# Attention's scores taken in float32 on halves of the array's rows, with TensorE's order written by hand

## The chip, the core and the metric

The kernel runs on one core of a Trainium2 chip. A core has TensorE (PE, the matrix array; its weight loads are shown as PEld), VectorE (DVE), ScalarE (ACT), GpSimd (POOL) and SyncE (SP, which here issues nearly all DMAs). The metric is the device time of one launch in microseconds (us).

## The reference

Three stages follow one another; everything is float32.

```python
# attention: B, H, S, D = 2, 8, 576, 64
scores = q @ k^T / sqrt(D)
x = log1p(|i-j|) / log1p(max(i, 1))          # depends on positions only
bias = relu(x * w1 + b1) @ w2                # hidden 32, one value per head
attn = softmax(scores + bias); out = attn @ v
# x = the heads side by side: (1152, 512)
# MoE: each token goes to its argmax expert of 8 (a capacity of 288 each):
y = relu(x @ w1[e]) @ w2[e], times the gate's probability
# a second layer: h = y @ w_in (512 -> 2048), leaky relu with alpha, @ w_out
```

## The kernel before

**Units.** Attention is done in 16 units (`pair(i)`): a pair of heads of one batch, and a set of query rows. Units 0 to 7 (phase 0) have two "big" row blocks of 128 rows (`ul` 0 and 1) and a "small" block in which 64 rows of both heads share the 128 partitions. Units 8 to 15 (phase 1) have the two big blocks alone. The big block has 576 keys for each of two heads. The list `UL` holds, in this order: the small blocks of units 0 to 2, their ul 0, their ul 1 (nine steps), then units 3 to 7, each big and then small, then units 8 to 15. The loop over `s` puts into one step the scores of entry s, the transposes of entry s - 1 and the values of entry s - 2.

**Scores.** `load(i)` brings q and k of a pair of heads, each stored twice over the partitions. `split(i)` makes of each a rounded part (DVE casts, L224 and L229) and a remainder (POOL subtracts, L225 and L230) in the type fp32r. `big(h, ul)` then forms the 128 x 576 scores of one head in four fp32r matmuls of 288 columns over all 128 rows of the array (L290); the two parts stand one above the other in those rows. The small block takes eight such matmuls (L274).

**Softmax and values.** `soft` adds the bias and takes the maximum in one DVE instruction (L262) and the exponential on ACT (L264). `stage_transpose` turns the result over on PE (L327, small: L309 and L314) in groups of up to four 128 x 128 blocks, `(0, 1)`, `(2, 3)`, `(4,)`, `(5, 6)`, `(7, 8)`, into one of two PSUM banks (`pt`); a copy by ACT or DVE (L298, L300) brings each group to SBUF. `stage_values` multiplies by v on halves of the array's columns (L352), and by `vd` over the whole array (L355).

**Bias.** There are 36 bias tiles k. Each needs four tensors `h` (128 x n, n from 576 down to 304; L169 on ACT, L171 on DVE or POOL, by `H_PLAN`), matmuls on four column tiles of the array (L175), an eviction in two instructions to `st` (L182 on ACT, L184 on DVE, by `EV_PLAN`), and a DMA into DRAM (`bd`). `load_bias` reads it back in the layout of the scores. Thirteen tiles are written ahead of the first scores (`PRE0` and `NB[0]`), the rest in the nine first steps and in units 3 to 7.

**PSUM.** The pool `pq` has two tiles of two banks each, for scores and bias tiles alike; `pt` and `pa` have two banks each.

**Order.** Each engine runs its own queue in order. The code above sets which work is written first, and a scheduler then chooses each engine's order from its own estimates. Behind attention come the routing (L406 and on, started in pieces when unit 11's values are done, `late`), the gather of the tokens by POOL (L495), the experts' products (L611 and on), and the second layer (L845 and L857).

## Time and profile before

| | |
|---|---|
| median of three runs | 421.54 us (421.21 to 425.41) |
| the profiled execution | 422.72 us |
| its span, first to last instruction | 421.0 us |
| mean granted clock of TensorE | 0.986 of 2.4 GHz |
| busy: PE, DVE, ACT, POOL | 94%, 75%, 57%, 27% of the span |

The busy shares are means over the whole span. Attention and what follows it have different limits, so the rows below are taken stage by stage.

### The profile page before, as it was taken

The page shows a single profiled execution, that of the slowest core. Times are in us where ns is not written, and L with a number is a line of the kernel's source. Part 1 is how long each engine was busy: PE and PEld are TensorE (multiplying, and loading weights), DVE is VectorE, ACT ScalarE, POOL GpSimd, SP SyncE. Part 2 cuts the span into 40 slices and gives each one's busy share as a digit, 9 for nine tenths or more (in the row PEclk, how much of TensorE's full clock was granted, in tenths as well). Part 3 has the DMA queues.
Part 4 walks back from the last instruction along what each step waited for, and adds up shares of the span by engine and source line. Part 5 has one row for each costly group of instructions (what it writes and reads, how often), then busy time and mean ns, then how long its engine had stood idle before and what let it go on. Part 6 is the DMA issues. An engine that isn't in the chain of part 4 may idle for free. (4 is left out here: it accounts for less than half of the span.)

```text
span 421.0 us, 7767 instructions
## 1 busy us (share of the span) xinstructions
PE 394.4 (94%) x2710; PEld 294.6 (70%) x2711; DVE 316.5 (75%) x723; ACT 239.4 (57%) x515; POOL 113.5 (27%) x99
## 2 busy tenths in 40 slices
PE   4689999989999999999998989999999999999993
PEld 2234544535787877786764789887898989897982
DVE  5889777697678777595977799832799998998440
ACT  4556646767666667566456333633577665665531
POOL 5732002342255556655242054001000000000003
PEclk9789999999999999999999999999999999999997
DMA  8847777777896889976149729929345644651003
GB/s 249 233 128 197 219 225 221 221 191 223 251 290 216 263 246 309 303 265 206 36 139 250 245 105 272 293 104 298 91 148 166 195 137 167 200 158 44 2 0 125
DMA packets 58059, 80.29 MB, mean 191 GB/s; under 512 B 10935, under 2 KB 37687, under 8 KB 58012
## 3 DMA queue, kind: packets, MB, share of 16 engines
q1 hardware_dynamic: 56828, 77.24, 60.5%
q0 software_dynamic: 1184, 2.48, 1.6%
q8 instruction: 23, 0.38, 0.4%
q14 instruction: 24, 0.20, 0.1%
HBM read 61.01 MB, written 20.09 MB: 193 GB/s over the span
## 5 line engine op out<-in xcount | busy, mean ns | idle before, releaser
L264 ACT ACTIVATE p<-p,mn 128x576 f32<-128x576 f32 x72 | 55.8, 775 | 32.6 <-DVE mn L262 32.1
L175 PE MATMUL bps<-h,c 128*32 128x512 f32 (+17 forms) x352 | 60.6, 520 | 13.4 <-DVE h L171 13.3
L171 DVE TENSOR_SCALAR h<-c 128x432 f32<-128x432 f32 (+17 forms) x108 | 54.5, 555 | 9.3 <-PE bps L175 9.1
L262 DVE CUSTOM_DVE_ANT_0 p<-sps,bias 128x576 f32<-128x576 f32 x72 | 53.7, 754 | 9.8 <-PE sps L290 5.2
L230 POOL TENSOR_TENSOR kk<-kr,kk 64x1216 fp32r<-64x1216 f32 x16 | 44.7, 2796 | 8.1 <-issue 6.3
L327 PE MATMUL t<-ident,p 128*128 128x128 f32 x288 | 46.0, 279 | 0.4 <-ACT PT L298 0.4
L175 PEld LDWEIGHTS bps<-h,c 128*32 128x32 f32 x352 | 17.1, 116 | 39.0 <-DVE h L171 17.3
L352 PE MATMUL av<-PT,vt 128*64 128x256 f32 (+1 forms) x304 | 42.8, 357 | 0.0
L327 PEld LDWEIGHTS t<-ident,p 128*128 128x128 f32 x288 | 32.9, 141 | 13.9 <-issue 5.5
L290 PE MATMUL sps<-kk,qh 128*128 128x288 f32 x120 | 39.4, 344 | 0.3 <-ACT st L182 0.3
L225 POOL TENSOR_TENSOR ql<-qr,qh 128x512 fp32r<-128x512 f32 x15 | 23.7, 1583 | 58.7 <-DVE qh L224 40.8
L298 ACT COPY PT<-t 128x512 f32<-128x512 f32 x51 | 29.0, 579 | 16.3 <-PE t L327 16.0
L889 POOL DMA_INDIRECT out<-orow,ti x5 | 4.9, 973 | 116.7 <-ACT orow L886 115.2
L845 PE MATMUL fg<-yh,w1h 128*128 128x304 f32 x120 | 36.3, 302 | 0.0
L845 PE MATMUL fg<-yh,w1l 128*128 128x304 f32 x120 | 36.2, 302 | 0.0
L845 PE MATMUL fg<-yl,w1h 128*128 128x304 f32 x120 | 36.2, 302 | 0.0
L182 ACT ACTIVATE st<-bps,c 128x527 f32<-128x527 f32 (+57 forms) x58 | 26.2, 501 | 16.2 <-PE bps L175 11.7
L290 PE MATMUL sps<-kk,ql 128*128 128x288 f32 x120 | 33.9, 298 | 0.0
L352 PEld LDWEIGHTS av<-PT,vt 128*64 128x64 f32 x304 | 21.2, 136 | 13.1 <-issue 7.5
L857 PE MATMUL facc<-w2h,hl 128*128 128x512 f32 (+1 forms) x75 | 29.8, 398 | 0.3 <-DVE hl L547 0.3
L857 PE MATMUL facc<-w2h,hh 128*128 128x512 f32 (+1 forms) x75 | 29.7, 396 | 0.0
L770 ACT ACTIVATE cv<-d 128x512 f32<-128x512 f32 x32 | 21.5, 675 | 14.1 <-DMA d<-in_win 7.2
(216 smaller groups left out, 927.4 us busy)
## 6 DMA issues: line engine op xcount, KB each, us to landing
bd<-st SPq DMA_DIRECT2D x36, 295.5 KB, 3.2
kr<-in_kT SPq DMA_DIRECT2D x16, 608.0 KB, 5.8
raw<-in_ew SPq DMA_DIRECT2D x16, 512.0 KB, 6.2
d<-in_win SPq DMA_DIRECT2D x16, 512.0 KB, 3.7
d<-in_wout SPq DMA_DIRECT2D x16, 512.0 KB, 3.7
bias<-bd SPq DMA_DIRECT2D x16, 288.0 KB, 4.6
vt<-in_vt SPq DMA_DIRECT2D x16, 256.0 KB, 4.7
bias<-bd SPq DMA_DIRECT2D x16, 256.0 KB, 4.3
```

The costliest lines, as they stand in the source:

```text
L171: (G if plan[c] == 'P' else V).tensor_scalar(h, tab[:, :n], psi[:, i:i + 1], 0.0, ALU.add, ALU.max)
L175: T.matmul(ps[32 * c:32 * c + 32, n0:n1], w2n, hs[c][:, n0:n1], start=True, stop=True)
L182: A.activation(d, src, AF.Copy, scale=rr[:, t:t + 1])
L230: G.tensor_tensor(kk[64:128], k[64:128], kk[64:128].bitcast(F32), ALU.subtract)
L262: V.tensor_tensor_reduce(out.rearrange("p (a b) -> p a b", a=2), ps[:, :, :288], bias.rearrange("p (a b) -> p a b", a=2), -0.125, 3.0e38, ...
L264: A.activation(out, out, AF.Exp, bias=mn, scale=-1.0, accum_out=acc)
L290: T.matmul(ps[:, nh, :288], qs[j][:, h, 128 * ul:128 * ul + 128], kk[:, k0:k0 + 288], start=j == 0, stop=j == 1)
L298: A.copy(o, i)
L327: T.transpose(t[:, jl, 128 * i:128 * i + 128], u.P[ul][:, 128 * j:128 * j + 128], ident)
L352: T.matmul(u.o[64 * h:64 * h + 64, :n], v[:, j, 64 * h:64 * h + 64], rhs(h, j), start=j == 0, stop=False, skip_group_check=True)
L845: T.matmul(ps, w[:, 128 * k:128 * k + 128], x[:, k, s], start=k + i == 0, stop=k + i == 5)
L857: T.matmul(acc[i][:m], h[:, r:r + m], w, start=f == 0 and j == 0, stop=f == NF - 1 and j == 2)
```

## The change

**Scores.** `split` is gone, with all casts and subtracts. q (128 x 320) and k (128 x 640) are loaded once, head 0 on partitions 0 to 63 and head 1 on 64 to 127, half the bytes of before. `big(ul)` forms the scores of both heads: four float32 matmuls of 288 columns, each over half of the array's rows (64), written so that one on the upper half is followed by one on the lower half; the heads go to two PSUM tiles (four banks). The small block does the same with 64 x 64 tiles of the array, both halves into one bank on different partitions.

**Bias.** `bias_h` writes the four `h` of a tile two tiles ahead (twelve buffers instead of six), all on DVE but one of eight up to tile 13, which ACT makes. All evictions are ACT's, and each stands right behind its tile's matmuls. `NB` and `EV` spread tiles and loads anew: `PRE0` 9 tiles, then 2, 2, 2, 3, 3, 3, 1, 1, 1 in the first nine steps, then 2 in each of units 3 to 7. There, one tile lies behind the transposes and one behind the values.

**Order.** `course()` is written under a manual schedule for PE: PE's order is the order of the code, `do()` by `do()`. The other engines stay with the scheduler. Big and small of one unit are one step (`SL`). The pieces of the routing are spread over more places. v has five buffers instead of four.

```diff
-H_PLAN = '322211000000016221010166000066000000'
-EV_PLAN = 'AAAAAAAAAAADAADDDDAAAAADAAAAAAAAAAAD'
-NB = (4, 0, 2, 4, 4, 3)
-EV = {0: [(0, 4, 1)], 1: [(1, 2)], 2: [(0, 0, 0)], 5: [(0, 0, 1), (0, 1, 1)], 6: [(0, 1, 0)]}
+NB = (2, 2, 2, 3, 3, 3, 1, 1, 1, 2, 2, 2, 2, 2)
+EV = {0: [(4, 1)], 2: [(0, 0)], 3: [(0, 1)], 5: [(1, 0), (1, 1)]}
...
+
+        def bias_h(k):
+
             t = (list(range(32, 36)) + list(range(32)))[k]
-            ps = pq.tile([128, 1024], F32, tag="pq", name="bps")
-            plan = ('DDDA', 'DDDD', 'DDAA', 'DADA', 'DAAA', 'PDDA', 'PDDD')[int(H_PLAN[k])]
-            hs = []
+            n = max(S - 16 * t, 16 * t + 16)
             for c in range(4):
-                h = bp.tile([128, S], F32, tag="h", name="h", bufs=6)[:, :n]
+                h = bp.tile([128, S], F32, tag="h", name="h", bufs=12)[:, :n]
                 i = t * 4 + c
-                if plan[c] == 'A':
+                if c == 3 and k % 2 == 0 and k < 14:
                     A.activation(h, tab[:, :n], AF.Relu, bias=psi[:, i:i + 1], scale=1.0)
                 else:
-                    (G if plan[c] == 'P' else V).tensor_scalar(h, tab[:, :n], psi[:, i:i + 1], 0.0, ALU.add, ALU.max)
-                hs.append(h)
+                    V.tensor_scalar(h, tab[:, :n], psi[:, i:i + 1], 0.0, ALU.add, ALU.max)
+                HS[k][2].append(h)
+
+        def bias_t(k):
+            if k == 0:
+                bias_h(0)
+                bias_h(1)
+            if k + 2 < NT:
+                bias_h(k + 2)
+            t, n, hs = HS.pop(k)
+            nf, nr = S - 16 * t, 16 * t + 15
+            ps = pq.tile([128, 1024], F32, tag="pq", name="bps")
             for n0, n1 in ((0, min(n, 512)), (512, n)):
                 for c in range(4 if n1 > n0 else 0):
                     T.matmul(ps[32 * c:32 * c + 32, n0:n1], w2n, hs[c][:, n0:n1], start=True, stop=True)
...
-                    d = st[:, o:o + src.shape[1]]
-                    if EV_PLAN[k % len(EV_PLAN)] == 'A':
-                        A.activation(d, src, AF.Copy, scale=rr[:, t:t + 1])
-                    else:
-                        V.tensor_scalar(d, src, rr[:, t:t + 1], None, ALU.mult)
...
-            pend.append(finish)
-            if len(pend) > 1:
-                pend.pop(0)()
+            st = bp.tile([128, PITCH], F32, tag="st", name="st", bufs=4)
+            for o, src in ((0, ps[:, nr:0:-1]), (nr, ps[:, 0:nf])):
+                A.activation(st[:, o:o + src.shape[1]], src, AF.Copy, scale=rr[:, t:t + 1])
...
-        RAW, KQV = {}, {}
...
-            q = kq.tile([128, 2, 320], F32, tag="qr", name="qr")[:, :, :w]
-            k = kq.tile([128, 1216], F32, tag="kr", name="kr")
-            v = ap.tile([128, 4, 128], F32, tag="vt", name="vt", bufs=4)
-            SY.dma_start(q, a["qT"][b, hp][:, :, 320 * ph:320 * ph + w])
+            q = kq.tile([128, 320], F32, tag="qr", name="qr", bufs=4)[:, :w]
+            k = kq.tile([128, 640], F32, tag="kr", name="kr", bufs=4)
+            v = ap.tile([128, 4, 128], F32, tag="vt", name="vt", bufs=5)
...
-        def split(i):
...
-                    V.tensor_copy(hi, x)
-                    G.tensor_tensor(lo, x, hi.bitcast(F32), ALU.subtract)
-
-            kk = (kq.tile([128, 1216], F32R, tag="bias", name="kk", bufs=9) if 2 <= i < EP else
-                  kq.tile([128, 1216], F32R, tag="kk", name="kk"))
-            V.tensor_copy(kk, k)
-            G.tensor_tensor(kk[64:128], k[64:128], kk[64:128].bitcast(F32), ALU.subtract)
-            KQV[i] = qs, kk, v
+            KQV[i] = q, k, v
...
-                unit(i, 1)
-            unit(i, 0)
+            return u
+
+
+        SL = [[unit(i, not uls, uls)] for uls in ((), (0,), (1,)) for i in range(EP)]
+        SL += [[unit(i, z) for z in ((0, 1) if i < 8 else (0,))] for i in range(EP, 16)]
 
         def soft(ps, bias, out, acc):
...
                 ps = pq.tile([128, 2, 512], F32, tag="pq", name="sps")
                 for nh in range(2):
-                    for n, (h, j) in enumerate(((0, 0), (0, 1), (1, 0), (1, 1))):
-                        k0 = 640 * h + 288 * nh
-                        T.matmul(ps[:, nh, :288], qz[u.i % 2][j][:, 2 * h:2 * h + 2], kk[:, k0:k0 + 288],
-                                 start=n == 0, stop=n == 3)
+                    for p in half:
+                        T.matmul(ps[p, nh, :288], q[p, 0:64], k[p, 64 + 288 * nh:352 + 288 * nh], start=True, stop=True)
...
-            def big(h, ul):
-                ps = pq.tile([128, 2, 512], F32, tag="pq", name="sps")
+            def big(ul):
+                ps = [pq.tile([128, 2, 512], F32, tag="pq", name="sps") for _ in range(2)]
+                c = q.shape[1] - 256 + 128 * ul
                 for nh in range(2):
-                    for j in range(2):
-                        k0 = 576 * h + 288 * nh
-                        T.matmul(ps[:, nh, :288], qs[j][:, h, 128 * ul:128 * ul + 128], kk[:, k0:k0 + 288], start=j == 0, stop=j == 1)
+                    for h, p in enumerate(half):
+                        k0 = 64 - 64 * h + 288 * nh
+                        T.matmul(ps[h][:, nh, :288], q[p, c:c + 128], k[p, k0:k0 + 288], start=True, stop=True)
                 row = 2 * u.ph + ul
-                soft(ps, BT[row, u.hp][:, h], u.P[ul][:, h * S:h * S + S], rs[u.b][:, row, 2 * u.hp + h:2 * u.hp + h + 1])
-
-            return [lambda h=h, ul=ul: big(h, ul) for h in range(2) for ul in u.uls]
+                for h in range(2):
+                    soft(ps[h], BT[row, u.hp][:, h], u.P[ul][:, h * S:h * S + S],
+                         rs[u.b][:, row, 2 * u.hp + h:2 * u.hp + h + 1])
+
+            return [lambda ul=ul: big(ul) for ul in u.uls]
...
-            tr = stage_transpose(UL[s - 1]) if 1 <= s <= NU else []
-            va = stage_values(UL[s - 2]) if s >= 2 else []
+                tr = sum(map(stage_transpose, ws), [])
+                va = sum(map(stage_values, xs), [])
+                nb = NB[s] if s < len(NB) else 0
...
+                do(tr)
+                do(sc)
+                if len(sc) == 2:
+                    do(tr, 3)
+                    more_bias(1)
+                    do(sc[1:])
+                    do(tr, 9)
+                    do(sc)
+                    do(va, 99)
+                    more_bias(nb - 1)
+                elif sc:
+                    step()
+                    do(tr, 2)
+                    step()
+                    do(va, 99)
+                    step()
+                    do(sc)
+                    do(tr, 9)
+                    step()
+                else:
+                    step()
+                    do(tr, 9)
+                    step()
+                    more_bias(nb and 1)
+                    do(va, 99)
+                    more_bias(nb - 1)
...
+                if xs and xs[0].i == 11:
+                    st = routing(0)
+                    late.extend([st[0:1], st[1:2], st[2:3], st[3:5], st[5:7], st[7:9], st[9:10], [st[10], st[11], second]])
+
+        with tc.manual_schedule(engines={ET.PE}):
+            course()
+        while late:
+            for f in late.pop(0):
+                f()
```

The names in the order below: `sps` are scores in PSUM, `t` transposed blocks in PSUM, `p` the softmax's result, `av` the values, `qh` and `ql` the rounded part and the remainder of q, `qr` and `kr` q and k as loaded. Square brackets tell whose work an instruction waits for (`DVE_49`: DVE's, `DMAHW`: a DMA's).

PE, in the last eight units (8 to 15), one unit before:

```order
L355 MATMUL av<-PT,vd_98 128x256
L290 MATMUL sps<-kk,qh 128x288
L290 MATMUL sps<-kk,ql 128x288
L290 MATMUL sps<-kk,qh 128x288
L290 MATMUL sps<-kk,ql 128x288
L327 MATMUL t_2113<-ident,p_1966 128x128
...
L290 MATMUL sps<-kk,qh 128x288
L327 MATMUL t_2166<-ident,p_2058 128x128
...
L290 MATMUL sps<-kk,ql 128x288
...
L352 MATMUL av<-PT,vt 64x256 x7
L355 MATMUL av<-PT,vd_98 128x256
L290 MATMUL sps<-kk,qh 128x288
```

PE, the same place after (`p_1760` is what the unit before left, `p_1848` and `p_1849` are ul 0 and ul 1 of this one):

```order
L323 MATMUL av<-PT,vt 64x256 x7
L326 MATMUL av<-PT,vd_98 128x256
L259 MATMUL sps<-kr,qr 128x288 [waits DVE_49] x2
L259 MATMUL sps<-kr,qr 128x288 x2
L298 MATMUL t_1908<-ident,p_1760 128x128 [waits DVE_49]
...
L298 MATMUL t_1914<-ident,p_1760 128x128 [waits Activation_49]
...
L298 MATMUL t_1934<-ident,p_1848 128x128 [waits DVE_49]
L298 MATMUL t_1934<-ident,p_1849 128x128 [waits Activation_49]
...
L259 MATMUL sps<-kr,qr 128x288 [waits DMAHW4_49,DMAHW3_49]
L259 MATMUL sps<-kr,qr 128x288 x3
```

Before, a head's scores stood between groups of transposes, one head at a time. Now both heads of a row block stand together, the second block behind the values, and four transposes of this unit's own softmax stand ahead of the next unit's scores.

DVE, in the last eight units, before and then after:

```order
L262 ISA p_2058,mn<-sps,bias 128x576
L262 ISA mn 128x1
L300 COPY xT_110<-av 128x256
L262 ISA p_2059,mn<-sps,bias 128x576
L262 ISA mn 128x1
L300 COPY PT<-t_2113 128x256
L262 ISA p_2058,mn<-sps,bias 128x576
L262 ISA mn 128x1
L262 ISA p_2059,mn<-sps,bias 128x576
L262 ISA mn 128x1
L300 COPY PT<-t_2139 128x512
L224 CAST qh<-qr 128x512
```

```order
L230 ISA p_1849,mn<-sps,bias 128x576
L230 ISA mn 128x1
L230 ISA p_1849,mn<-sps,bias 128x576
L230 ISA mn 128x1
L271 COPY PT<-t_1914 128x512
L230 ISA p_1925,mn<-sps,bias 128x576
L230 ISA mn 128x1
L230 ISA p_1925,mn<-sps,bias 128x576
L230 ISA mn 128x1
L271 COPY PT<-t_1958 128x256
L271 COPY xT_102<-av 128x256
```

Behind the second block's two `p_1849` now stands the copy of four transposed blocks (`t_1914`), which the next transposes need, since there are two banks for them; the casts of q and k are gone.

DVE, from the start to the first softmax, before and then after:

```order
L171 TENSOR_SCALAR h<-c_84 128x528 x2
L171 TENSOR_SCALAR h<-c_84 128x544 x2
L224 CAST qh<-qr 128x512
L229 CAST kk<-kr 128x1216
L171 TENSOR_SCALAR h<-c_84 128x560 x2
L224 CAST qh<-qr 128x512
L224 CAST qz_102<-qr 128x2x64
L224 CAST qz_104<-qr 128x2x64
L229 CAST kk<-kr 128x1216
...
L171 TENSOR_SCALAR h<-c_84 128x432 x4
L262 ISA p_439,mn<-sps,bias_354 128x576
```

```order
L163 TENSOR_SCALAR h<-c_84 128x528 x3
L163 TENSOR_SCALAR h<-c_84 128x544 x4
L163 TENSOR_SCALAR h<-c_84 128x560 x3
L163 TENSOR_SCALAR h<-c_84 128x576 x7
...
L163 TENSOR_SCALAR h<-c_84 128x448 x3
L163 TENSOR_SCALAR h<-c_84 128x432 x4
L230 ISA p_369,mn<-sps,bias_356 128x576
L230 ISA mn 128x1
L230 ISA p_421,mn<-sps,bias_356 128x576
L230 ISA mn 128x1
```

Before, 41 `h` and eight casts stand ahead of the first `p`; after, 49 `h` and no cast.

## Rows read from the trace of the kernel before

**Rows 1.** Busy time by stage: start:end, us, engines' busy time, PE clock, DMA share, GB/s.

```profile
core 0: us, PE busy (x) PEld busy (x) DVE busy (x) ACT busy (x) POOL busy (x), PEclk, DMA share, GB/s
0.00:39.00 39.00, 27.43 (x169) 10.51 (x170) 30.73 (x54) 20.68 (x40) 18.32 (x31) 0.91 0.68 197
39.00:106.70 67.70, 65.40 (x465) 33.66 (x465) 52.83 (x139) 44.07 (x94) 19.08 (x15) 1.00 0.79 219
106.70:153.00 46.30, 46.29 (x390) 37.28 (x388) 34.13 (x88) 28.61 (x67) 20.95 (x17) 1.00 0.81 257
153.00:228.00 75.00, 74.56 (x524) 54.27 (x522) 56.07 (x154) 45.69 (x101) 35.66 (x19) 1.00 0.69 218
228.00:421.00 193.00, 180.68 (x1172) 158.87 (x1170) 142.76 (x293) 100.38 (x214) 19.48 (x19) 0.99 0.49 153
```

**Rows 2.** Timeline of DVE, front: start, us, engine, line, operation [idle before].

```profile
5.42 1.72 DVE L171 TENSOR_SCALAR h<-c 128x528 f32<-128x528 f32 x4
...
12.05 2.83 DVE L229 CAST kk<-kr 128x1216 fp32r<-128x1216 f32 x1 [1.12 <-DMA kr<-in_kT]
14.80 7.21 DVE L171 TENSOR_SCALAR h<-c 128x576 f32<-128x576 f32 x8
...
40.30 0.76 DVE L262 CUSTOM_DVE_ANT_0 p<-sps,bias 128x576 f32<-128x576 f32 x1
```

**Rows 3.** Timeline of POOL, front.

```profile
16.71 2.85 POOL L230 TENSOR_TENSOR kk<-kr,kk 64x1216 fp32r<-64x1216 f32 x1
```

**Rows 4.** Timeline of PE: four places from the first transposes to unit 8's scores.

```profile
42.12 0.66 PE L309 MATMUL t<-ident,p 128*128 128x128 f32 x4
...
55.93 0.37 PE L290 MATMUL sps<-kk,qh 128*128 128x288 f32 x1
...
104.52 0.77 PE L290 MATMUL sps<-kk,qs 128*128 128x288 f32 x4
...
153.12 0.40 PE L290 MATMUL sps<-kk,qh 128*128 128x288 f32 x1
```

**Rows 5.** DMA issues: KB each, median us from issue to landing.

```profile
bd<-st SPq DMA_DIRECT2D x36, 295.5 KB, 3.2
...
bias<-bd SPq DMA_DIRECT2D x16, 288.0 KB, 4.6
```

**Rows 6.** Timeline of ACT, front: an eviction.

```profile
39.05 0.91 ACT L182 ACTIVATE st<-bps,c 128x143 f32<-128x143 f32 x2 [1.03 <-PE bps L175]
```

**Rows 7.** Timeline of PE, phase 0: a bias tile, then eight transposes and two heads' scores.

```profile
111.03 1.06 PE L175 MATMUL bps<-h,c 128*32 128x512 f32 x8
112.02 0.40 PE L290 MATMUL sps<-kk,qh 128*128 128x288 f32 x1
...
126.73 1.07 PE L327 MATMUL t<-ident,p 128*128 128x128 f32 x8
127.56 0.38 PE L290 MATMUL sps<-kk,qh 128*128 128x288 f32 x1
...
128.79 0.66 PE L309 MATMUL t<-ident,p 128*128 128x128 f32 x4
```

**Rows 8.** Timeline of PE, one unit of the last eight.

```profile
170.34 0.70 PE L355 MATMUL av<-PT,vd 128*128 128x256 f32 x2
170.69 0.48 PE L290 MATMUL sps<-kk,qh 128*128 128x288 f32 x1
...
176.05 1.94 PE L352 MATMUL av<-PT,vt 128*64 128x256 f32 x14
177.92 0.70 PE L355 MATMUL av<-PT,vd 128*128 128x256 f32 x2
178.27 0.48 PE L290 MATMUL sps<-kk,qh 128*128 128x288 f32 x1
```

**Rows 9.** Timelines of PE, DVE and ACT, from one head's last score matmul on.

```profile
171.27 0.29 PE L290 MATMUL sps<-kk,ql 128*128 128x288 f32 x1
171.71 0.76 DVE L262 CUSTOM_DVE_ANT_0 p<-sps,bias 128x576 f32<-128x576 f32 x1 [0.21 <-PE sps L290]
...
174.14 0.69 DVE L300 COPY PT<-t 128x512 f32<-128x512 f32 x1
...
172.51 0.78 ACT L264 ACTIVATE p<-p,mn 128x576 f32<-128x576 f32 x1 [2.58 <-DVE mn L262]
173.19 0.18 ACT L264 ACTIVATION_READ_ACCUMULATOR p<-p,mn 128x1 f32 x1
173.28 0.56 ACT L298 COPY PT<-t 128x512 f32<-128x512 f32 x1
```

**Rows 10.** Timelines of POOL and PE, attention's end.

```profile
216.84 0.98 POOL L495 DMA_INDIRECT xd<-xr,ci  x1 [0.30 <-issue]
...
227.87 0.74 PE L593 MATMUL xjT<-ident,xj 96*128 96x96 f32 x7
...
231.63 0.53 PE L611 MATMUL g<-xh,w1h 128*128 128x288 f32 x2
```

More of the change, by code (lines that the diff above doesn't have):

```diff
@@ L106, in build @@
             G.memset(vd[b], 0.0)
-        qz = [[bp.tile([128, 4, 64], F32R, name=f"qz{i}{j}") for j in range(2)] for i in range(2)]
-        for z in qz[0] + qz[1]:
-            G.memset(z.bitcast(F32), 0.0)
         xT = [xp.tile([128, 4, 640], F32, tag=f"xT{b}", name=f"xT{b}") for b in range(B)]
@@ L248, in unit @@
             u.last = small == 0 and 1 in uls
-            UL.append(u)
-        for uls in ((), (0,), (1,)):
-            for i in range(EP):
-                unit(i, not uls, uls)
-        for i in range(EP, 16):
-            if i < 8:
-                unit(i, 1)
-            unit(i, 0)
+            return u
+        SL = [[unit(i, not uls, uls)] for uls in ((), (0,), (1,)) for i in range(EP)]
+        SL += [[unit(i, z) for z in ((0, 1) if i < 8 else (0,))] for i in range(EP, 16)]
         def soft(ps, bias, out, acc):
@@ L266, in stage_scores @@
         def stage_scores(u):
-            qs, kk, _ = KQV[u.i]
+            q, k, _ = KQV[u.i]
+            half = [slice(64 * h, 64 * h + 64) for h in range(2)]
             def small():
@@ new lines, in course, with do, step @@
+        def course():
+            nonlocal raw
+            for k in range(PRE0):
+                more_bias(1)
+                if k in (1, 3):
+                    load(2 + k // 2)
+            load_bias(4, 0)
+            load_vd(1)
+            for s in range(NU + 2):
+                us, ws, xs = [SL[z] if 0 <= z < NU else [] for z in (s, s - 1, s - 2)]
+                u = us[0] if us else None
+                for x in EV.get(s, ()):
+                    load_bias(*x)
+                if u and u.i < 8 and u.last and u.i % 2 == 0 and u.hp < 3:
+                    if u.i > 0:
+                        for w in (0, 1):
+                            load_bias(w, u.hp + 1)
+                    if u.hp < 2:
+                        load_bias(4, u.hp + 2)
+                if u and u.i == 7:
+                    load_bias(2, 0)
+                    load_bias(2, 1)
+                if u and 8 <= u.i < 11:
+                    load_bias(3, u.hp + 1)
+                    if u.hp < 2:
+                        load_bias(2, u.hp + 2)
+                if u and u.i == 2 and u.small:
+                    SY.dma_start(c1, a["c1"])
+                if u and 8 <= u.i < 15:
+                    clear(3 * u.i - 24)
+                sc = sum(map(stage_scores, us), [])
+                if u and u.last and u.i + 2 < 16 and u.i + 2 not in KQV:
+                    load(u.i + 2)
+                tr = sum(map(stage_transpose, ws), [])
+                va = sum(map(stage_values, xs), [])
+                nb = NB[s] if s < len(NB) else 0
+                def do(fs, n=1):
+                    for f in fs[:n]:
+                        f()
+                    del fs[:n]
+                def step():
+                    if late:
+                        for f in late.pop(0):
[4 more added lines that the diff above has]
+                    do(tr, 3)
+                    more_bias(1)
+                    do(sc[1:])
[19 more added lines that the diff above has]
+                    more_bias(nb - 1)
+                if u and u.i == 7:
+                    load_bias(3, 0)
+                if raw is None and u and u.i == 8:
+                    for b in range(B):
+                        rest_sums(b)
+                if xs and xs[0].i == 8:
+                    right.close()
+                    raw = ctx.enter_context(tc.tile_pool(name="raw", bufs=1, side="right"))
+                if xs and xs[0].i == 11:
+                    st = routing(0)
+                    late.extend([st[0:1], st[1:2], st[2:3], st[3:5], st[5:7], st[7:9], st[9:10], [st[10], st[11], second]])
```

107 lines of the change are left out of this document (15 added, 92 removed).

## Prediction

> **What bounds the kernel now.** I read the busy time by stage first [rows 1]. It shows two limits. From 39 us on PE is the engine that sets the pace: 65.40 of 67.70 us busy, then 46.29 of 46.30, then 74.56 of 75.00. In the first 39 us it is busy for 27.43 only, at a granted clock of 0.91, and DVE for 30.73. So work taken from DVE and POOL can pay in the first 39 us directly, and behind that only where PE gets less to do. The last 193 us are not touched by the change. They start when the tokens of attention are routed, so a gain in attention counts as far as it reaches the first job's product.
>
> The timeline of DVE's front shows what holds the start [rows 2]. Four h of 528 columns took 1.72 us, .43 each. The eight of 576 columns took 7.21 us, .90 each, and one cast of k took 2.83 us. Both lie beside POOL's subtract, of which one took 2.85 us [rows 3]. The first softmax came at 40.30, the first transposes at 42.12, the first wide scores at 55.93, unit 2's last scores at 104.5, unit 8's first at 153.1 [rows 2, 4]. These are the marks that I move one after the other.
>
> **The front.** Before the first softmax DVE now has 49 h and no cast, and POOL subtracts nothing. Undisturbed h of 576 to 432 columns, from .43 for 528 columns [rows 2], are some .40 each: 49 x .40 = 19.6 us from 5.4, so DVE is free at 25.0. The softmax needs the small bias, which is stored and read back: eviction, store and load took .91, 3.2 and 4.6 us [rows 5, 6], its tiles are the first four, and its read stands behind five later stores in SP's queue. I allow 1.3 us for that: the first softmax at 26.3, the first transposes 1.9 behind it as before, at 28.2 instead of 42.12: 14 us gained. The big blocks' bias for unit 0 ends with tile 12, evicted near 32.6; 3.2 + 4.6 later, at about 41, the first wide softmax can run, against some 56: 15 us gained.
>
> The six steps behind that hold three bias tiles in each of the first three, one in each of the others. In the first three ACT is the longest chain: two exponentials of .78 + .18 [rows 9], a copy of .56, three evictions of .91 [rows 6] and the hand-over to the next scores, which need the second PSUM tile, make 7.1 us each. The other three take 5.3 each by the same sum with one eviction and PE's own waits. Unit 2's last scores would end at 41 + 3 x 7.1 + 2 x 5.3 = 72.9, against 105.2 [rows 4]: 32 us gained. Part of this is work put off: ten of 36 bias tiles are left for later.
>
> **What scores cost on PE.** A float32 matmul of 256 columns on the whole array takes two passes of some .215 us: `vd`'s two ran from 177.92 to 178.27 with the change of shape [rows 8], and fourteen passes of `av`, in pairs on two column halves at once, lie in 1.87 us. For 288 columns that is .48. Two heads on row halves at once make two pairs for each block, .97 us. Before, two heads took eight fp32r matmuls in 1.2 us (127.56 to 128.79 [rows 7]), each .13. So the scores cost PE about the same, if the halves run at once; no row of before has row halves. The nearest rows, `av` on column halves, say that they do, and I take that. The other bound is one after the other, 1.93 us for a block.
>
> The Trainium skill speaks for it too ("TensorE: Matmul & The Clock Gate", Part 3): matmuls on different row groups run concurrently, and four row tiles gave 3.07 times the speed of one. Were two halves to reach that 77%, a pair would take .63 us instead of .48, and 64 pairs on the path would add some 9 us, 423 in all: an estimate from that page, which no run here shows.
>
> Of those 1.87 us, one `av` matmul alone and three pairs are 4 x .43 = 1.72; the rest, .15, is a change of the array's shape. I take .16. The order counts 160 of them in attention on either side, so they cancel.
>
> **Units 3 to 7.** PE's work in one is: scores 1.92, small 2 x .48 = .96, 23 transposes of .104 (eight in .83 [rows 7]) 2.4, values 1.72 + .43, `vd` .53, twelve changes 1.9, two bias tiles of .75 (.99 at 512 columns [rows 7], less for fewer) 1.5: 11.5 us. To this come waits that the hand-written order makes. The second transposes wait for a copy that stands behind two softmax instructions of .76 on DVE; the small block's last transpose waits in the same way; the next unit's scores wait until ACT has evicted the bias tile. From these durations [rows 6, 9] I count 1.2 to 1.4, .5 and .4. The five units then take 10.1, 11.7, 13.8, 13.8 and 12.5 us, the first ones with fewer tiles and cover from work left over. With 5.3 for the step before, unit 8's first scores come at about 140, against 153.1: of 32 us, 19 are given back here, and 13 to 14 stay.
>
> **The last eight units.** Before, a unit took 7.58 us, which is PE's work with hardly a gap: from `vd` at 170.34 to `vd` at 177.92 [rows 8]. After: scores 1.92, 18 transposes 1.9, values 1.72, `vd` .43, six changes .96, together 6.9. But the next unit's first four transposes now need the exponential of this unit's second block, and a bank that DVE's copy frees behind two softmax instructions. Counted from the last score matmul: the first softmax ends .44 + .76 after that matmul's start, the second .75 later, the copy .69 after that [rows 9]. PE has only the eight transposes, .83 us [rows 7], to put between. That leaves about 1.3 us without work. I take 8.3 us for a unit, 9.1 and 9.3 for the first two, where the pipeline turns from one kind of unit to the other; against 7.58 that loses 5.6 in the eight and some 3 more with the two slow ones and the routing pieces. Attention would end at 219.5 instead of about 227.9, a gain of 8.4. Behind its end the gather and its transposes lie open (216.84, then 227.87 and 231.63 [rows 10]); since routing starts behind the same unit and less attention covers it, I charge 1.5. The first product comes at 224.7 instead of 231.6: 7 us gained.
>
> The casts, subtracts and half of q's and k's bytes that are gone beyond the front count for nothing: POOL was no engine that PE waited for there, and DMA was busy for 0.69 to 0.81 of the stages [rows 1]. If that cover is wrong, it is a gain.
>
> **Sum.** 422.72, the profiled execution, less 7 is 415.7. It stood 1.2 above the median, so I predict 414 us (-1.8%). A change of under 1%, 4.2 us, can't be told from none here.
>
> **Rivals.**
> First, the row halves run one after the other. Then each pair costs .48 more. 80 pairs make 38.4; those of the front partly lie beside ACT's chain, so some 32 count, and the time is 414 + 32 = 446. It decides from .09 more per pair on, since 7 / 80 = .09 uses up the gain. For it: no row shows row halves, and both heads' weights must be loaded into one array. Against it: the column halves run at once in every unit.
>
> Second, the waits of the hand-written order don't appear, since DVE and ACT are free (56 and 46 of 75 us busy [rows 1]) and choose an order that I did not follow closely enough. Then PE's work alone counts: 1.3 x 8 + 1.8 in the last eight, 5.6 in units 3 to 7, some 5 in the three slow steps of the front: 23 us less, 391.
>
> Third, the small block's two halves write one PSUM bank and are held apart: 16 pairs x .48 = 7.7, so 422, no change. Against it: four column tiles write one bank at once in each bias tile (eight passes in .99 [rows 7]). The Trainium skill has this as a rule ("TensorEngine Tiling (Array Packing)", Restrictions and Gotchas): different row tiles cannot access the same PSUM bank at the same time. No row here has that case.
>
> Fourth, the front gains 3 us instead of 14: the bias round trip of 8.7 us or PE's clock, 0.91 there [rows 1, 5, 6], holds the first softmax back, or PE's order, fixed, waits for each tile's eviction. The 32 us shrink to some 21, and the time is 425. Against it: DVE's queue is the later of the two by my count.
>
> **How the numbers follow.** My forecast, 405 to 424, has .47: .32 faster by over 1%, .13 within it, .02 slower. The first rival has .14, all slower. The second has .20, all faster. The third has .10: .08 within 1%, .02 slower. The fourth has .09: .05 within, .04 slower. Faster .52, same .26, slower .22. The range from 386 to 429 leaves out the first rival and the fastest of the second, together less than .2.
>
> **What would show it.** In the profile after, the first transposes should stand near 28, unit 2's last scores end near 73, unit 8's first scores near 140, a last unit take 8.3 us with about 1.3 us of PE's idle time ahead of its first transposes, released by DVE or ACT. Two score matmuls of different halves should start within some .05 us of each other and a block's four end within 1.1 us. A row half that starts only when the other has ended makes the whole forecast wrong. So would PE without any gap in the last eight units, on the other side.

## The result, and the profile after

The change made no gain: 425.54 us (median of 20 runs, 422.64 to 428.36) against 421.38 for the kernel before (20 runs), a ratio of 1.0093 with a 95% interval of 1.0071 to 1.0115. Slower by nearly 1%, where I had forecast 1.8% faster. The profiled execution has a span of 423.6 us and a mean clock of 0.972. Here and below, medians are over all executions, and ratios leave out those that were more than 1.5% above the fastest of their kernel.

Busy time of the changed kernel in three of the stages of [rows 1] (columns as there; the last one is longer by its span):

```profile
0.00:39.00 39.00, 26.33 (x226) 10.27 (x227) 26.43 (x74) 20.41 (x44) 4.18 (x20) 0.87 0.75 221
...
153.00:228.00 75.00, 62.85 (x468) 40.62 (x464) 40.38 (x120) 36.44 (x84) 7.33 (x7) 1.00 0.26 79
228.00:423.60 195.60, 183.87 (x1164) 161.33 (x1164) 144.27 (x293) 100.75 (x214) 16.61 (x17) 0.96 0.48 153
```

From 153 to 228 us PE was busy for 74.56 of 75 us before; now it is idle for 12 us there. And the last stage, whose instructions are not changed, has a clock of 0.96 instead of 0.99.

Timeline of PE in the changed kernel, at the places of [rows 4, 8, 10]: start, us, engine, line, operation, count, [idle before, released by].

```profile
19.83 1.19 PE L243 MATMUL sps<-kr,qr 64*64 64x288 f32 x8
...
30.05 1.09 PE L280 MATMUL t<-ident,p 128*128 128x128 f32 x4 [3.25 <-ACT p L232]
...
71.43 1.37 PE L259 MATMUL sps<-kr,qr 64*128 64x288 f32 x8
...
88.75 0.66 PE L298 MATMUL t<-ident,p 128*128 128x128 f32 x4 [0.70 <-DVE PT L271]
...
93.06 0.30 PE L285 MATMUL t<-ident,dup 128*128 128x128 f32 x1 [0.68 <-DVE PT L271]
...
138.84 1.24 PE L259 MATMUL sps<-kr,qr 64*128 64x288 f32 x8
...
149.69 1.24 PE L259 MATMUL sps<-kr,qr 64*128 64x288 f32 x8
...
172.23 1.24 PE L259 MATMUL sps<-kr,qr 64*128 64x288 f32 x8
173.40 1.09 PE L298 MATMUL t<-ident,p 128*128 128x128 f32 x8
175.69 0.66 PE L298 MATMUL t<-ident,p 128*128 128x128 f32 x4 [1.21 <-DVE PT L271]
176.28 1.24 PE L259 MATMUL sps<-kr,qr 64*128 64x288 f32 x8
...
184.14 0.66 PE L298 MATMUL t<-ident,p 128*128 128x128 f32 x4 [1.11 <-DVE PT L271]
184.72 1.24 PE L259 MATMUL sps<-kr,qr 64*128 64x288 f32 x8
...
193.27 1.24 PE L259 MATMUL sps<-kr,qr 64*128 64x288 f32 x8
194.44 1.28 PE L377 MATMUL lgT<-xT,c 128*32 128x512 f32 x16
...
204.89 1.24 PE L259 MATMUL sps<-kr,qr 64*128 64x288 f32 x8
...
225.30 0.82 PE L564 MATMUL xjT<-ident,xj 96*128 96x96 f32 x8
229.59 0.90 PE L564 MATMUL xjT<-ident,xj 96*128 96x96 f32 x4 [3.46 <-DVE xl L518]
...
232.28 0.85 PE L582 MATMUL g<-xh,w1h 128*128 128x288 f32 x2
```

The lead over the kernel before can be read off. At the first transposes it is 42.12 - 30.05 = 12.1 us, at unit 2's last scores 105.2 - 72.7 = 32.5 (their end, where the next instruction starts), at unit 8's first scores 153.12 - 138.84 = 14.3. At attention's end (the transposes `xjT` that follow the last values, 227.87 and 225.30) it is 2.6. At the first product of the experts it is -0.7, at the end of the span -2.6. The front did as forecast; the lead is lost behind unit 8, in two places: 11.7 us in the last eight units, and 5.2 behind attention's end (3.2 of them ahead of the first product).

In the last eight units one unit takes 176.28 to 184.72, 8.4 us, against 7.58 [rows 8]; of it 1.11 is the wait that the row at 184.14 shows, behind DVE. The unit before it has the same wait at 175.69, 1.21 us, and there DVE's timeline reads:

```profile
173.59 0.76 DVE L230 CUSTOM_DVE_ANT_0 p<-sps,bias 128x576 f32<-128x576 f32 x1 [0.83 <-PE sps L259]
...
174.95 0.69 DVE L271 COPY PT<-t 128x512 f32<-128x512 f32 x1
```

The copy at 174.95 frees the bank; it stands behind the two softmax instructions, the first at 173.59, of the block whose scores began at 172.23.

At attention's end, the timeline of ACT and the clock in two stretches behind it (columns as in [rows 1]):

```profile
225.62 1.04 ACT L517 CAST w1h<-raw 128x1024 fp32r<-128x1024 f32 x1 [4.99 <-DMA raw<-in_ew]
```

```profile
225.00:230.00 5.00, 1.54 (x13) 1.26 (x13) 3.72 (x6) 4.38 (x6) 2.27 (x2) 0.89 1.03 352
230.00:239.00 9.00, 9.00 (x43) 5.94 (x42) 3.78 (x6) 2.17 (x5) 0.00 (x0) 0.50 0.92 278
```

The first weights are split only when attention has ended. (The row names a DMA as what ended ACT's idle time; the section on 256 bytes comes back to that.) PE waits 3.46 us for the splits that follow, and then runs for 9 us at the lower of its two clocks.

### The profile page after: what moved, and what is told of

The parts are those of the page before. It is cut to its first block, busy times and chain, and to the rows that moved or that the text cites. A ratio compares the mean times of both kernels' runs of the same rounds, so it can differ in the third digit from the quotient of the medians.

```text
span 423.6 us, 7637 instructions
## 1 busy us (share of the span) xinstructions
PE 377.3 (89%) x2710; PEld 272.7 (64%) x2711; DVE 284.0 (67%) x698; ACT 229.3 (54%) x505; POOL 30.0 (7%) x50
## 3 DMA queue, kind: packets, MB, share of 16 engines
q1 hardware_dynamic: 54780, 70.16, 53.4%
## 5 line engine op out<-in xcount | busy, mean ns | idle before, releaser
L163 DVE TENSOR_SCALAR h<-c 128x528 f32<-128x528 f32 (+17 forms) x137 | 51.1, 442 | 10.4 <-PE bps L177 10.2
L177 PE MATMUL bps<-h,c 128*32 128x512 f32 (+17 forms) x352 | 38.1, 515 | 11.1 <-DVE h L163 5.3
L259 PE MATMUL sps<-kr,qr 64*128 64x288 f32 x256 | 45.8, 432 | 0.9 <-ACT st L180 0.9
L180 ACT ACTIVATE st<-bps,c 128x527 f32<-128x527 f32 (+35 forms) x72 | 32.4, 505 | 16.4 <-issue 6.9
L259 PEld LDWEIGHTS sps<-kr,qr 64*128 64x128 f32 x256 | 25.4, 186 | 13.0 <-ACT st L180 4.5
L323 PE MATMUL av<-PT,vt 128*64 128x256 f32 (+1 forms) x304 | 31.9, 352 | 0.0
L828 PE MATMUL facc<-w2l,hh 128*128 128x512 f32 (+1 forms) x75 | 29.5, 393 | 0.0
L177 PEld LDWEIGHTS bps<-h,c 128*32 128x32 f32 x352 | 10.1, 116 | 24.5 <-ACT st L180 7.7
L816 PEld LDWEIGHTS fg<-yh,w1h 128*128 128x128 f32 x120 | 22.6, 188 | 1.0
L816 PEld LDWEIGHTS fg<-yl,w1h 128*128 128x128 f32 x120 | 22.5, 188 | 0.6
```

What stands on the lines that cost most here:

```text
L163: V.tensor_scalar(h, tab[:, :n], psi[:, i:i + 1], 0.0, ALU.add, ALU.max)
L177: T.matmul(ps[32 * c:32 * c + 32, n0:n1], w2n, hs[c][:, n0:n1], start=True, stop=True)
L180: A.activation(st[:, o:o + src.shape[1]], src, AF.Copy, scale=rr[:, t:t + 1])
L259: T.matmul(ps[h][:, nh, :288], q[p, c:c + 128], k[p, k0:k0 + 288], start=True, stop=True)
L323: T.matmul(u.o[64 * h:64 * h + 64, :n], v[:, j, 64 * h:64 * h + 64], rhs(h, j), start=j == 0, stop=False, skip_group_check=True)
L816: T.matmul(ps, w[:, 128 * k:128 * k + 128], x[:, k, s], start=k + i == 0, stop=k + i == 5)
```

## The experiments

Ratios are against the kernel before, measured beside each kernel. Three theories were tried in turn. **Theory 1**: PE's hand-written order has nothing to do where it waits. **Theory 2**: two heads' scores at once, which fill all four score banks, make the unit longer in any order. **Theory 3**, formed after the first eight runs: the extra v buffer delays the first weights.

### Scores ahead of the transposes

```diff
-                do(tr)
-                do(sc)
+                if len(sc) == 2:
+                    do(sc)
+                    do(tr)
+                else:
+                    do(tr)
+                    do(sc)
```

> The changed kernel, but in the last eight units the scores of a unit's first row block stand ahead of the four transposes of the unit before, not behind them. Theory 1 (what was lost in the last eight units are PE's waits of the fixed order: 1.2 us in each unit ahead of those four transposes, behind DVE's copy): the scores need only the two softmaxes, which end some .7 us before that copy, so the wait falls from 1.2 to about .5, a unit takes 7.9 us instead of 8.5, and the kernel about 421 instead of 425.5. Rival (DVE, ACT and the four banks that one row block's scores fill set the unit's period in any order): the wait only moves to the scores, a unit keeps 8.5, and the kernel 425.5.

Measured: 438.46 us (435.53 to 443.03), ratio 1.0371 (1.0287 to 1.0455). Worse than either theory had it. PE in one of its units, to the start of the next:

```profile
174.07 1.24 PE L259 MATMUL sps<-kr,qr 64*128 64x288 f32 x8
...
176.27 1.91 PE L259 MATMUL sps<-kr,qr 64*128 64x288 f32 x8
...
180.79 0.44 PE L298 MATMUL t<-ident,p 128*128 128x128 f32 x2 [1.59 <-ACT PT L269]
...
183.66 1.24 PE L259 MATMUL sps<-kr,qr 64*128 64x288 f32 x8
```

A unit takes 9.59 us. The scores at 176.27 take 1.91 instead of 1.24, which fits a wait for their banks (the row names none), and the transposes behind them wait 1.59 for ACT's copies, which now stand behind the exponentials of the block just scored (exponentials at 178.64 and 179.41, copies from 180.17). The order of PE also decides what is queued where on ACT and DVE, and that I had not followed.

### The routing in six places

```diff
-late.extend([st[0:1], st[1:2], st[2:3], st[3:5], st[5:7], st[7:9], st[9:10], [st[10], st[11], second]])
+late.extend([st[0:2], st[2:4], st[4:6], st[6:8], st[8:10], [st[10], st[11], second]])
```

> The changed kernel, but the pieces of the routing are grouped as in the kernel before: six places instead of eight. Theory (the end of attention is followed by 3.5 us in which PE waits, and by 9 us at half the clock, because the experts' weights are loaded behind the scatter in SP's queue, and the scatter ends two places too late): the last scatter goes out about 4 us earlier than 218.25, the gap closes, the clock stays at full speed, 3 to 5 us less: 421 to 422. Rival (the gap is DVE's own work on the weights, whenever they come; denser pieces stretch units 14 and 15 by as much): within 1 us of 425.5.

Measured: 429.04 us, ratio 1.0155 (1.0084 to 1.0225). PE in unit 14:

```profile
193.23 1.24 PE L259 MATMUL sps<-kr,qr 64*128 64x288 f32 x8
...
201.17 0.65 PE L413 MATMUL rk<-run,ones 128*128 128x40 f32 x2 [2.02 <-DVE run L406]
...
202.55 3.68 PE L323 MATMUL av<-PT,vt 128*64 128x256 f32 x16
...
206.81 1.00 PE L259 MATMUL sps<-kr,qr 64*128 64x288 f32 x6
```

With two pieces at one place PE stands in its fixed order until DVE has made the second one's input, 2.02 us, and then has the lower clock (0.50 from 201.17 to 206.16 us; 16 passes of the values in 3.68 us instead of 1.95). The unit takes 13.6 us instead of 11.6. The theory itself was not put to the test: the last scatter went out at 218.58, no earlier than the 218.25 of the changed kernel. By the ratios the time is not told apart from that of the changed kernel (1.0071 to 1.0115).

Both edits together:

> Both edits: scores of the first row block ahead of the transposes in the last eight units, and the routing in six places. If both theories hold the gains add to 7 to 9 us, 417 to 418, below the kernel before (421.4). If attention's end and the routing's chain run side by side and the later one counts, the sum is less than the two together: 420 to 421.

Measured: 442.66 us, ratio 1.0471 (1.0382 to 1.0561), 17.1 us more than the changed kernel by the medians, near the 12.9 and 3.5 of the two edits alone.

### PE's order by the scheduler

```diff
-        with tc.manual_schedule(engines={ET.PE}):
-            course()
+        course()
```

> The changed kernel with PE's order left to the scheduler; scores, bias and all else as changed. Theory 1 (the hand-written order is what loses): the last eight units run with little idle time on PE, near 7.3 us each instead of 8.5, units 3 to 7 nearer 12 than 14, and the kernel lands at 410 to 416. Rival (the new scores' use of PSUM, DVE and ACT is what loses): unit periods as in the changed kernel, 8.3 or more, and 424 to 428; an order that the scheduler makes with wrong estimates of row halves could be slower yet.

Measured: 423.5 us, ratio 1.0068 (1.0027 to 1.011), 2 us less than the hand-written order by the medians, though the intervals overlap. One unit of the last eight starts its scores at 160.76 and the next at 168.89, 8.1 us:

```profile
162.95 1.42 PE L259 MATMUL sps<-kr,qr 64*128 64x288 f32 x4
...
164.89 0.76 PE L259 MATMUL sps<-kr,qr 64*128 64x288 f32 x4
```

The scheduler splits a block's scores in two, and the first four passes take 1.36 us, twice their .7, which fits a wait for a bank (the row names none). This spoke for theory 2: another order also stays above 7.58.

### The scores of before from unit 8 on

```diff
+            if u.ph:
+                return [lambda h=h, ul=ul: big1(h, ul) for h in range(2) for ul in u.uls]
             return [lambda ul=ul: big(ul) for ul in u.uls]
...
         with tc.manual_schedule(engines={ET.PE}):
-            course()
+            course(0, 14)
+        course(14, NU + 2)
```

`big1` is `big` of the kernel before, with its own loads and splits. PE's order is the scheduler's from unit 8 on, the routing has its six places, and v has four buffers.

> The changed kernel up to unit 7, and from unit 8 on the scores of the kernel before: casts and subtracts, four fp32r matmuls over the whole array, one head at a time, PE's order by the scheduler, the routing in the grouping of before. h has eight buffers and v four, to make room. Theory 2 (the two heads' scores at once, which fill all four score banks and release two softmaxes together, are what loses in the last eight units, and the fixed order beside it): units 8 on take 7.6 us as in the kernel before, so the lead of 14 us at unit 8 is kept to the end: 407 to 410. Rival (the lead would be lost in any case, because the routing, the weights or DMA of the end are tied to something else): 415 or more.

Measured: 418.55 us, ratio 0.9873 (0.9818 to 0.9928). From the third of these units on one takes 7.58 us again. But unit 8 starts 5.7 us later than in the changed kernel (144.54 instead of 138.84; h and k have fewer buffers here), and the passage to the other kind of unit takes 3.5 us more than in the kernel before. So it is not a clean test of theory 2; the next one is.

### Values on both sides of the second block's scores

```diff
                     step()
-                    do(va, 99)
+                    do(va, 2)
                     step()
                     do(sc)
                     do(tr, 9)
+                    do(va, 99)
                     step()
```

> The changed kernel, but in the last eight units only two of the five steps of the values stand between the scores of the two row blocks; the other three and vd stand behind the transposes that follow the second block, ahead of the next unit's first transposes. Moving the scores themselves made units longer (9.6 us instead of 8.5), since copies of ACT then stood behind the next block's exponentials. If what PE lacks at that place is only work that depends on nothing near (theory 1), the values cover the wait of 1.2 us, two more changes of shape cost .4, and a unit takes 7.7 instead of 8.5 us; five undisturbed units give 4 us, 421 to 422. If the chain of scores, two softmaxes, exponentials and copies is as long as the unit (rival), the wait appears at the second block's scores instead and the time stays within 1.5 of 425.5.

Measured: 415.89 us, ratio 0.9836 (0.9771 to 0.9901): 9.6 us less than the changed kernel by the medians, 2.6% by the ratios. In the profiled executions 8.0 us of it lie between unit 8's first scores and attention's end (78.5 instead of 86.5); behind the first product 2.3 are gained as well, where this execution had a shorter stretch at the lower clock. PE in one of the last eight units:

```profile
164.49 1.24 PE L259 MATMUL sps<-kr,qr 64*128 64x288 f32 x8
165.66 0.87 PE L298 MATMUL t<-ident,p 128*128 128x128 f32 x6
166.47 1.08 PE L323 MATMUL av<-PT,vt 128*64 128x256 f32 x8
167.48 1.24 PE L259 MATMUL sps<-kr,qr 64*128 64x288 f32 x8
168.65 1.09 PE L298 MATMUL t<-ident,p 128*128 128x128 f32 x8
169.67 1.08 PE L323 MATMUL av<-PT,vt 128*64 128x256 f32 x8
170.69 0.70 PE L326 MATMUL av<-PT,vd 128*128 128x256 f32 x2
171.22 0.60 PE L298 MATMUL t<-ident,p 128*128 128x128 f32 x4
171.75 1.24 PE L259 MATMUL sps<-kr,qr 64*128 64x288 f32 x8
```

No row has a wait, and a unit takes 7.26 us, less than the 7.58 of before. Theory 2 falls: two heads at once can run without a gap. Theory 1 holds in this form: work that depends on nothing near has to stand behind the scores of each of the two blocks; the changed kernel had put all of the values behind the first. How short each portion may be was not tested. Waits stay in unit 8 (1.21) and in the units that hold the routing (1.11 at most).

### The routing half a unit earlier

```diff
                     do(va, 99)
                     step()
+                    if xs[0].i == 11:
+                        st = routing(0)
+                        late.extend([...])
                     do(sc)
...
-                if xs and xs[0].i == 11:
-                    st = routing(0)
-                    late.extend([...])
```

> The changed kernel, but the routing starts within the step in which unit 11's values are written, half a unit earlier: its first product stood at 194.44, 5.2 us behind the end of these values at 189.2, while the kernel before had its own at 190.57 though it was 7 us later in attention there. Theory (the scatter and what SP loads behind it set when the experts' first product can start, not attention's end): the last scatter goes out some 4 us earlier than 218.25, the 3.5 us of waiting behind attention's end shrink to under 1 and the stretch at half the clock goes: first product at 228 to 229 instead of 232.3, 420 to 421 in all. Rival (DVE's own splits of the weights make the gap whenever the weights come, or the routing stretches units 13 to 15 as much as it starts earlier): 424.5 to 427.

Measured: 426.6 us, ratio 1.0102 (1.0044 to 1.016), not told apart from the changed kernel. The last scatter of POOL went out at 213.39 instead of 218.25, yet PE's wait behind attention's end stayed, 3.54 us:

```profile
229.80 0.90 PE L564 MATMUL xjT<-ident,xj 96*128 96x96 f32 x4 [3.54 <-DVE xl L518]
```

The loads behind the scatter went out 4.9 us earlier too. So the scatter and these loads do not set this wait. With the split values:

> Both edits: values split around the second block's scores, routing half a unit earlier. If both theories hold: 416 to 418. If only the routing's chain counts, as the early start alone. If only the waits count, as the split alone.

Measured: 420.51 us, ratio 0.9949 (0.9911 to 0.9987), 4.6 more than the split alone by the medians: the earlier routing has no gain. In the profiled executions attention ends 1.5 us later (218.25 instead of 216.74), and 4.1 us more lie behind the first product, from where the clock is at 0.76 up to 245 us.

### 256 bytes ahead of the weights

All kernels with the wait of 3.5 us had in common that the first cast of weights stands right behind attention's last values. In the kernel before (timeline of ACT) it does not:

```profile
221.78 1.05 ACT L546 CAST w1h<-raw 128x1024 fp32r<-128x1024 f32 x1
```

That is 6 us ahead of attention's end, and in the run with the scores of before from unit 8 on, which has four v, it stood at 217.16 with the end at 223.25. By the code, a partition of the pool `ap` holds two `vd` of 2 KB, four v of 2, four p of 4.5 and two PT of 9: 48 KB; with five v it is 50. The pool `my`, which takes its place, has two tiles of 22.5 KB, two of 2.4 and two of 64 bytes, 49.9 KB, and the weights come behind it. So with five v the first weight tile would reach over the end of `ap` by some 130 bytes, and its cast would have to wait until PE has read PT for the last time. The row of the changed kernel names a DMA, but its weights were asked for 19.6 us before the cast; in the run with the earlier routing, the row of the same cast names PE's last read of PT:

```profile
225.76 1.05 ACT L517 CAST w1h<-raw 128x1024 fp32r<-128x1024 f32 x1 [6.39 <-PE av L326]
```

```diff
         my = pool(ctx, "my")
+        my.tile([128, 64], F32, name="pad")
```

> The changed kernel with one unused tile of 64 columns (256 bytes a partition) ahead of the pool that holds the experts' split weights; no work is added. Theory 3: five v buffers instead of four make attention's pool ap 50 KB a partition, and the weights' first tile begins at 49.8 KB, so the first cast of weights must wait until attention's last values have read their tile; it started at 225.62 us, right behind them, though its weights had been loaded for long, while before it started 6 us ahead of attention's end. With the tile the cast goes out by 219, PE's wait of 3.46 us behind attention's end falls to about 1.5 as before, and PE does not fall to half its clock there: 4 us less, 421 to 422. Rival (the weights come too late, or DVE and ACT have the work of the splits to do at that place in any case): within 1 us of 425.5.

Measured: 420.92 us, ratio 0.9972 (0.9946 to 0.9997), 4.6 us less than the changed kernel by the medians and 1.2% by the ratios, whose intervals lie apart, through an unused tile. ACT and then PE:

```profile
217.01 1.04 ACT L517 CAST w1h<-raw 128x1024 fp32r<-128x1024 f32 x1
```

```profile
225.71 0.82 PE L564 MATMUL xjT<-ident,xj 96*128 96x96 f32 x8
227.36 0.55 PE L564 MATMUL xjT<-ident,xj 96*128 96x96 f32 x4 [0.83 <-DVE xl L518]
...
228.84 0.53 PE L582 MATMUL g<-xh,w1h 128*128 128x288 f32 x2
```

The cast goes out 8.6 us earlier, the wait is .83, and the clock from 225 to 245 us is 1.00. That the two tiles overlap is shown by this; that the fifth v is what made them overlap follows from the sizes in the code, and no run has the changed kernel with four v and nothing else. With the split values:

> The values split around the second block's scores (415.9 measured for that alone) and the unused tile. Theory 3: the first product comes 2 to 3 us earlier and a short stretch at half the clock goes, 412 to 413. Rival: 415.5 to 416.5.

Measured: 413.4 us, ratio 0.979 (0.9753 to 0.9826), 2.5 us less than the split alone by the medians, as expected; the intervals of the two overlap.

### The waits of units 3 to 7

On top of the split values and the unused tile:

```diff
-                    do(tr, 3)
+                    do(tr, 2)
+                    do(va, 2)
+                    do(tr, 1)
                     more_bias(1)
                     do(sc[1:])
+                    do(tr, 2)
+                    do(va, 3)
                     do(tr, 9)
```

> As the one with the split values and the unused tile, and in units 3 to 7 two pieces of the values stand ahead of the transposes (5, 6), and three ahead of the small block's last transpose, where PE waited .70 and .68 us in each unit for a copy of DVE. If only covered work was missing, five units lose 1.4 us each: about 6 us less than without, 406 to 407. If the copies only come later (ACT's evictions and exponentials set the unit's period of 12 to 14 us), the time stays within 2 us of the one without.

Measured: 409.97 us, ratio 0.9685 (0.9646 to 0.9724), the fastest of all: 3.1% under the kernel before, but 3.4 us gained where 6 were expected. PE in unit 4:

```profile
89.74 0.66 PE L298 MATMUL t<-ident,p 128*128 128x128 f32 x4
...
94.22 0.27 PE L285 MATMUL t<-ident,dup 128*128 128x128 f32 x1
...
96.61 0.93 PE L177 MATMUL bps<-h,c 128*32 128x432 f32 x8 [0.95 <-DVE mn L230]
```

The two waits of .7 are gone, and the unit's second bias tile, with less ahead of it, waits .95 behind a softmax of DVE. Unit 4 is no shorter for it (85.95 to 98.06, against 85.42 to 97.35 in the changed kernel); units 4 to 7 together take 51.2 us, against 53.4 without this edit.

### A block's scores head by head

Also on top of the split values and the unused tile:

```diff
-                for nh in range(2):
-                    for h, p in enumerate(half):
+                for h, p in enumerate(half):
+                    for nh in range(2):
```

> As the one with the split values and the unused tile, but a row block's four matmuls are written head by head (two of the upper half, then two of the lower), not in turn. If row halves overlap only with their neighbour in PE's order, only the middle two run at once, and a block takes 1.45 us instead of .97: .48 more in each of 32 blocks, of which some 22 lie on PE's path, 10 to 15 us slower than without. If PE holds several in flight and overlaps them whatever their order: no difference. The first head's softmax may start earlier, which gives back up to .4 us a block where a softmax is waited for.

Measured: 415.92 us, ratio 0.9842 (0.9779 to 0.9905), not told apart from the one without (0.979, 0.9753 to 0.9826).

```profile
164.40 1.25 PE L259 MATMUL sps<-kr,qr 64*128 64x288 f32 x8
165.58 0.87 PE L298 MATMUL t<-ident,p 128*128 128x128 f32 x6
```

A block takes 1.18 us, as in turn (164.49 to 165.66 above). Eight passes of .24 one after the other would be 1.92. So the halves overlap in either order, and the 10 to 15 us that the other case would have cost are not there.

## Why the prediction was wrong

**The front was right.** Forecast were the first transposes at 28.2, unit 2's last scores at 72.9 and unit 8's first at 140; they came at 30.05, 72.7 and 138.84. The 32 us gained and the 18 given back in units 3 to 7 (19 forecast) are there. The waits for DVE's copies there are .70 and .68 us (rows at 88.75 and 93.06), smaller than the 1.2 to 1.4 and .5 that I had counted. The fourth rival, a front that gains 3 us instead of 14, did not come, but part of its mechanism did: PE waits 1.77 and 1.15 us for ACT's evictions ahead of 25 us, DVE's h wait for PE in turn, and the first softmax came at 28.25 instead of 26.3.

**Row halves run at once**, as taken: a block in 1.17 us with its changes of shape. The first rival, halves one after the other, falls. So does the third, halves held apart by one bank: the small block's eight passes take from 19.83 to some 21.0 as well, .24 a pair. The Trainium skill says that different row tiles cannot access one PSUM bank at the same time ("TensorEngine Tiling (Array Packing)", Restrictions and Gotchas); the trace does not agree for this case, where the two halves write different partitions of the bank, .24 us a pair as with two banks. (The price of a pass, .215 us for 256 columns, comes out of the `av` rows; `vd`'s row [rows 8] has .35 us for two passes and does not give it.)

**Where the 9.6 us lie.** By the forecast the span is 421.0 - 7 = 414.0 us; it was 423.6. Unit 8 began 1.2 us earlier than forecast; the last eight units took 7.0 longer, the stretch from attention's end to the first product 1.8, and what follows it 1.9. So two steps failed, and the first is the larger.

**The first step that failed is the sum of the last eight units: 86.5 us from unit 8's first scores to attention's end, where I had 79.5.** The mechanism was the one named, a wait of 1.1 to 1.2 us (about 1.3 forecast) for the copy behind two softmax instructions. But the sum leaves out a term of its own: it says that 5.6 us are lost in the eight units "and some 3 more" with the two slow ones and the routing pieces, and then takes only 14 - 5.6 = 8.4 as the gain at attention's end. With the 3 the forecast would have been about 417. The rest are sizes. PE's work without the wait is 7.3 us, not 6.9: 8.4 less 1.1. Unit 8 took 10.85 (138.84 to 149.69), not 9.1, and unit 9 9.5, not 9.3. Unit 14 took 11.6 (193.27 to 204.89), and from its start to attention's end it is 32.0 us, where 79.5 leaves 27.9 when the units before it are taken off. Unit 14's routing matmuls are 3.2 us of work there, and its waits (.66 and .54) add up to no more than those of the other units; with the routing in six places, waits of 1.12 and 2.02 for its inputs come on top.

**The second step that failed is the tail, "I charge 1.5", and here it was the mechanism.** Between attention's end and the first product lie 7.0 us (225.30 to 232.28) instead of 3.8 before and 5.2 forecast, and behind it PE runs at the lower clock, which costs 1.9 us more to the end (191.3 instead of 189.4 from the first product on). The reason given there, less attention to cover the routing, was not the cause: the routing half a unit earlier changed nothing. The cause is that the first weight tile lay over memory of attention that is read to the end: 256 bytes give 4.6 us back. By the code it is the fifth v buffer that puts it there, an edit that I had put at nothing without naming what it moves. With the 256 bytes alone the kernel is at 0.9972 of the kernel before: the tail made the small loss, and the last eight units ate up the gain.

**The second rival, no waits, 391 us**, was the wrong way for this kernel, but its mechanism is real: a few lines of PE's order take away the waits of units 9 to 13, and the last eight units take 78.5 us. With the 256 bytes that makes 413.4; that this is next to the 414 that I had forecast for the kernel as it was is chance.

## What to carry to other kernels

In an order written by hand, count for each wait the independent work that stands ahead of it, and share it out; the same values in two portions instead of one were worth 2.6%. Moving an instruction on one engine can also move its consumers in the other engines' queues: putting scores earlier cost 2.8%. When a pool grows, look at what is allocated in its place afterwards: here a tile that by the code reaches some 130 bytes into memory that is read to the very end made its first writer wait for that end. And when a sum is long, check that every term named in it is also taken off.

## What was not expected of the hardware

PE fell to the lower of its two clocks at waits of 2.02 us (the six places) and 3.46 us (attention's end), and stayed there for at least 9 us in the latter case; after the wait of .83 it did not. The length of one wait does not tell it alone: with the scores ahead of the transposes the clock stayed at 1.00 from 189 to 200 us behind a wait of 2.19, and with the earlier routing it was 0.50 from 218.2 to 221.5 us behind waits of no more than 1.11, so that 16 passes of the values took 2.93 us instead of 1.95:

```profile
219.53 2.93 PE L323 MATMUL av<-PT,vt 128*64 128x256 f32 x16
```

Two row halves overlap whether their matmuls are written in turn or two and two (1.17 and 1.18 us a block), so the order within a block made no difference to its length here.
